# A new hand-written order and other load order in a kernel of two attention and MLP layers

## The chip, the cores and the metric

The kernel runs on one core of one Trainium2 chip. The metric is device time in microseconds; the value of a kernel is the median of its runs. Before the change it is 461.99 us, the median of 3 runs (460.26 to 463.19).

A core has five engines that run side by side, each through its own list of instructions in order: TensorE (PE in the profile, with its weight loads as PEld), VectorE (DVE), ScalarE (ACT), GpSimd (POOL) and SyncE (SP), which issues the transfers (DMAs) here. Engines wait for one another by semaphores.

## The reference, cut to what matters

One sequence of 2048 tokens with 512 features passes twice through an attention layer and an MLP layer, with the same weights both times. Everything is bfloat16.

```python
def _A_ref(x, wqkv, wo):
    H = 32; Dh = D // H; W = 256
    qkv = (x @ wqkv).reshape(B, S, 3, H, Dh).transpose(2, 0, 3, 1, 4)
    q, k, v = qkv[0], qkv[1], qkv[2]
    scores = jnp.einsum("bhqd,bhkd->bhqk", q, k) * (Dh ** -0.5)
    mask = (idx[:, None] - idx[None, :] >= 0) & (idx[:, None] - idx[None, :] < W)
    p = _softmax(jnp.where(mask[None, None], scores, -1e9), axis=-1)
    o = jnp.einsum("bhqk,bhkd->bhqd", p, v)
    return o.transpose(0, 2, 1, 3).reshape(B, S, D) @ wo

def _B_ref(x, w1, b1, w2, b2):
    h = _gelu(jnp.einsum("bsd,df->bsf", x, w1) + b1)
    return jnp.einsum("bsf,fd->bsd", h, w2) + b2

x = x + _A_ref(_layernorm(x), A_wqkv, A_wo)
x = x + _B_ref(_layernorm(x), B_w1, B_b1, B_w2, B_b2)
x = x + _A_ref(_layernorm(x), A_wqkv, A_wo)
x = x + _B_ref(_layernorm(x), B_w1, B_b1, B_w2, B_b2)
```

There are 32 heads of 16 features, a sliding window of 256 keys, and 1792 hidden features in the MLP. Without the structure of the window the projections, the output projection and the MLP hold most of the matrix work.

## The kernel before

**Tiles and stages.** The 2048 tokens are 16 tiles of 128; the two passes make 32 of them, and two tiles make a block, so there are 16 blocks. The residual stream stays in `X` on the chip, and so do all weights. For a tile, `layernorm` (line 932) takes statistics on VectorE (939 and 941), adds epsilon (943), takes the reciprocal root on GpSimd (946) and normalizes on VectorE (949). The normalized tile must then be transposed: early tiles on TensorE (36), with a copy out on VectorE (922) or ScalarE (924); later ones by a VectorE transpose of 32 x 32 pieces into `xs_` (958), four writes to a scratch tensor in memory (967) and one read back (973), into `xnTA` for attention or `xnTB` for the MLP. `by_dma` (565) says which tiles go that way. A read back waits until the last users of its buffer have finished.

`lnq` and `kv` (1006 and 1034) are a block's two LayerNorms and its projections from the Q, K and V blocks of `Wqkv_sb`. `attention` (1081) makes score visits: a visit is 16 or 24 small matmuls of 32 rows by 64 columns on TensorE, which run side by side on parts of the array, followed by two exponentials on ScalarE (1124). Masks (1145) run on VectorE or GpSimd, then come matmuls with V (64 rows by 17 columns), which also sum the softmax, then VectorE work (1210 to 1220) and the output projection (1245). `mlp` (1267) handles jobs of two or four tiles, `JOBS` at line 582. A block's keys also meet queries of the next block, so the first scores need the projection of block 1, that is of tiles 2 and 3.

TensorE is used in three ways: whole array (f), score pieces (r) and V pieces (c). ScalarE has to load another function table between exponential and gelu.

**What sets the order.** The code adds about 3,400 nodes to a planner, each with an engine, an estimated duration, what it reads and what it writes. A node may have a second form on another engine. The list `ORDER` (line 636) then gives the order by hand: each entry is a node's number, and a negative one (`-47`) means node `~(-47)`, that is 46, in its second form. `follow` (248) walks down the list and sets an estimated start for every node. With these estimates it picks the PSUM banks of each result, and the estimated times decide at two places what the program waits for and where: they rank the semaphore waits (`op`, 89), and `spread` (136) moves a second or third wait of a matmul onto an earlier matmul, when the estimate says that the event is past by then. Nothing else of the estimates reaches the chip. Each engine issues its nodes in list order.

**The loads.** Node 18 loads `X` tiles 0 and 1 (256 KB); 19, 20 and 22 are the K, Q and V blocks of the weight (512 KB each); 21 is `X` tiles 2 and 3 (256 KB); 23 is the first MLP bias; 24, 25 and 26 are the other tiles of `X`; 27 is the output weight, 28 the second MLP bias, 29 and 30 the MLP weights. The code adds them in that order of numbers. The order in which SyncE issues them is that of the list, which before the change has 18, 21, 20, 19, 22. `load` (883) gives each an estimated duration, from the time of its issue and its size.

Of the kernel before, what the change touches and what calls it, by code (L numbers as in the profile page):

```python
# [518 lines left out]
def bass_interleave_layers__sliding_block__dense_activation_gelu__prompt_kernel(  # L519
# [11 lines left out]
    Bb, S, D = A_x.shape  # L531
# [61 lines left out]
    with ExitStack() as kctx:  # L593
        S_ = _Sched(nc, kctx)

        def sb(name, shape, dtype=dt.bfloat16):
# [283 lines left out]
        sp_t = [0.0, 0.0]  # L880
        landing = {}

        def load(fn, writes, kb, issue=500.0, behind=()):

            i = sp_t[0]
            for n in behind:
# [42 lines left out]
        def quads(name):  # L929
            return ["%s_%d" % (name, q) for q in range(4)]  # L930
# [453 lines left out]
```

## Time and profile before

| | us |
|---|---|
| median of 3 runs | 461.99 |
| lowest, highest | 460.26, 463.19 |
| the profiled execution, its own time | 458.59 |
| its span from first to last instruction | 456.9 |

The granted clock of TensorE is 1.00 in all stretches. The 40 slices of the span show how the engines' shares move; each digit is a tenth of a slice of 11.4 us:

```profile
PE   7997899999889999999999999999999999999997
DVE  5999997889996888988989799998888878687302
ACT  2899999998998989899997999988978798875352
```

TensorE is nearly full from the second third on, ScalarE in the first third. The costliest groups are the exponentials and the two MLP matmuls; a group line has the kernel's line, the engine, what is written and read, the count, then the busy time and the mean duration in ns, and last the idle time before it:

```profile
L1124 ACT ACTIVATE E<-ps 128x1024 bf16<-128x1024 f32 x304 | 286.0, 1052 | 29.2 <-PE ps L32 28.3
L32 PE MATMUL ps<-W_sb,gT 128*128 128x512 bf16 (+1 forms) x462 | 117.7, 374 | 0.0
L32 PE MATMUL ps<-xnTB,W_sb 128*128 128x512 bf16 (+1 forms) x560 | 116.8, 337 | 0.0
```

Busy time of an engine is the union of its records. Matmuls overlap, so the mean of one is longer than the spacing between two.

### The profile page before, as it was taken

To read this page: it belongs to the slowest core of one execution; us is meant where nothing else is said; L and a number is where in the kernel's file an instruction comes from. 1 tells how busy PE (TensorE), PEld (TensorE's weight loads), DVE (VectorE), ACT (ScalarE), POOL (GpSimd) and SP (SyncE) were. 2 spreads that over 40 slices of the span, in tenths; PEclk is the share of its full clock that TensorE was granted. 3 is DMA by queue.
4 is the path that set the end of the run, shared out by engine and by line. 5 is a ranking of instruction groups with operands and counts; after the bars stand their busy time and mean duration, and the time that the engine had idled before them with its cause. 6 is when DMAs were issued, how large, how long until landed. Compare 5 with 4: busy or idle time off the path is not lost.

```text
span 456.9 us, 19399 instructions
## 1 busy us (share of the span) xinstructions
PE 438.8 (96%) x8738; PEld 233.2 (51%) x8738; DVE 374.2 (82%) x759; ACT 388.5 (85%) x463; POOL 221.8 (49%) x256
## 2 busy tenths in 40 slices
PE   7997899999889999999999999999999999999997
PEld 3564464654444444655435545545454554454675
DVE  5999997889996888988989799998888878687302
ACT  2899999998998989899997999988978798875352
POOL 5377665832668556562455536644434512270500
PEclk9999999999999999999999999999999999999999
DMA  7670000001031022402230122412130021003101
GB/s 230 215 261 3 4 4 3 4 3 37 6 66 29 16 39 61 70 14 42 46 75 8 23 42 47 87 16 51 25 87 13 6 46 37 26 3 84 57 24 46
DMA packets 63902, 22.35 MB, mean 49 GB/s; under 512 B 49740, under 2 KB 63308, under 8 KB 63820
## 3 DMA queue, kind: packets, MB, share of 16 engines
q1 hardware_dynamic: 63820, 21.12, 19.8%
q8 instruction: 68, 1.11, 1.0%
q14 instruction: 14, 0.11, 0.1%
HBM read 13.50 MB, written 7.60 MB: 46 GB/s over the span
## 4 chain that ended last, share of the span: by engine, by line
PE 71%; ACT 25%; DVE 2%; DMA 1%; issue 0%; SPq 0%; POOL 0%; DVEq 0%
PE ps L32 70%; ACT E L1124 18%; ACT gT L1291 2%; ACT gT L1282 1%; ACT L1124 1%; DMA scr_x<-xs_ 1%; ACT L1282 1%; DMA X<-in_A_x_dram 1%; DVE TT L1210 1%; PE ps L36 0%; DVE stat L939 0%; ACT QT L924 0%; ACT xnTA L924 0%; ACT L1291 0%; SPq L967 0%
## 5 line engine op out<-in xcount | busy, mean ns | idle before, releaser
L1124 ACT ACTIVATE E<-ps 128x1024 bf16<-128x1024 f32 x304 | 286.0, 1052 | 29.2 <-PE ps L32 28.3
L1145 POOL TENSOR_TENSOR E<-E,mask 128x512 bf16<-128x512 bf16 (+1 forms) x122 | 126.0, 1047 | 103.9 <-DVE E L1145 41.4
L32 PE MATMUL ps<-W_sb,gT 128*128 128x512 bf16 (+1 forms) x462 | 117.7, 374 | 0.0
L32 PE MATMUL ps<-xnTB,W_sb 128*128 128x512 bf16 (+1 forms) x560 | 116.8, 337 | 0.0
L32 PEld LDWEIGHTS ps<-xnTB,W_sb 128*128 128x128 bf16 x560 | 51.1, 98 | 43.6 <-ACT E L1124 3.5
L32 PE MATMUL ps<-xnTA,Wqkv_sb 128*128 128x256 bf16 x512 | 70.5, 273 | 2.5 <-DVE veps L943 1.6
L32 PE MATMUL ps<-QT,KT 32*64 32x320 bf16 (+4 forms) x2976 | 64.8, 258 | 7.4 <-ACT E L1124 5.4
L946 POOL TENSOR_TENSOR rstd<-veps,mhalf 128x1 f32<-128x1 f32 x64 | 36.7, 576 | 67.2 <-DVE veps L943 67.1
L1291 ACT ACTIVATE gT<-ps,b1T 128x512 bf16<-128x512 f32 (+1 forms) x92 | 48.7, 588 | 22.3 <-PE ps L32 22.1
L1003 DVE TENSOR_TENSOR X<-X,ps 128x512 bf16<-128x512 bf16 x63 | 42.7, 682 | 28.6 <-PE ps L32 28.1
L32 PEld LDWEIGHTS ps<-W_sb,gT 128*128 128x128 bf16 x462 | 40.8, 98 | 44.0 <-issue 5.7
L1145 DVE TENSOR_TENSOR E<-E,mask 128x512 bf16<-128x512 bf16 (+1 forms) x140 | 52.3, 406 | 11.0 <-ACT E L1124 10.6
L32 PEld LDWEIGHTS ps<-xnTA,Wqkv_sb 128*128 128x128 bf16 x512 | 46.5, 98 | 22.6 <-issue 3.3
L32 PEld LDWEIGHTS ps<-QT,KT 32*64 32x64 bf16 x2976 | 27.4, 103 | 53.9 <-ACT E L1124 35.4
L32 PE MATMUL ps<-E,Va 64*17 64x128 bf16 (+3 forms) x3872 | 49.3, 230 | 2.8 <-POOL E L1145 0.5
L32 PEld LDWEIGHTS ps<-E,Va 64*17 64x17 bf16 x3872 | 39.4, 85 | 21.0 <-PE ps L32 7.5
L1254 POOL TENSOR_TENSOR X<-X,b2b 128x512 bf16<-128x512 bf16 x32 | 36.7, 1153 | 22.5 <-DVE E L1145 11.5
L939 DVE BATCH_NORM_STATS2 stat<-X 128x6 f32<-128x512 bf16 x64 | 43.5, 684 | 2.8 <-DMA X<-in_A_x_dram 2.2
L1210 DVE STREAM_TRANSPOSE TT<-ps 128x1024 f32<-128x1024 f32 x32 | 39.8, 1243 | 6.0 <-PE ps L32 5.4
L1043 DVE TENSOR_TENSOR KT<-ps,parmask 128x1024 bf16<-128x1024 f32 x32 | 38.6, 1214 | 3.7 <-PE ps L32 3.5
L32 PE MATMUL ps<-Wo_sb,OT 128*128 128x512 bf16 x128 | 35.4, 381 | 0.1
L32 PE MATMUL ps<-Wqkv_sb,xnTA 128*128 128x512 bf16 x128 | 35.4, 381 | 0.0
(50 smaller groups left out, 319.4 us busy)
## 6 DMA issues: line engine op xcount, KB each, us to landing
W_sb<-in_B_w_dram SPq DMA_DIRECT2D x2, 1792.0 KB
scr_x<-xs_ SPq DMA_DIRECT2D x104, 32.0 KB, 1.6
xnTB<-scr_x SPq DMA_DIRECT2D x26, 128.0 KB, 2.7
scr_q<-xs_ SPq DMA_DIRECT2D x64, 32.0 KB, 2.2
xnTA<-scr_q SPq DMA_DIRECT2D x16, 128.0 KB
out_dram<-X SPq DMA_DIRECT2D x15, 128.0 KB, 1.8
Wqkv_sb<-in_A_wqkv_dram SPq DMA_DIRECT2D x3, 512.0 KB, 6.9
X<-in_A_x_dram SPq DMA_DIRECT2D x3, 512.0 KB, 5.7
```

What stands on the lines that cost most here:

```text
L32: return self.e.matmul(*a, **k)
L939: add("dve", lambda e, B: e.bn_stats(stat6[:, k6, :], X[:, t, :]), 590, reads=["X%d" % t], writes=["st%d" % k6], prio=prio)
L946: add("pool", lambda e, B: e.tensor_tensor(out=rstd[:, k : k + 1], in0=veps[:, k : k + 1], in1=mhalf[:], op=ALU.pow), 535, reads=["ve%d" % ...
L1003: add("dve", lambda e, B: e.tensor_tensor(out=X[:, t, :], in0=X[:, t, :], in1=ps[:, B[g][0], :], op=ALU.add), d_psum(512), reads=["X%d" % ...
L1043: add("dve", lambda e, B, g=g, i=i: e.tensor_tensor(out=KT[:, kb, :, 2 * i : 2 * i + 2, :].rearrange("p a c q -> p a (c q)"), in0=ps[:, B[ ...
L1124: add("act", lambda e, B, g_=g_, gi=gi: e.activation(E[:, 2 * gi : 2 * gi + 2, e0 : e0 + 512], ps[:, B[g_][0] : B[g_][0] + 2, :], AF.Exp, ...
L1145: op = lambda e, B, Ew=Ew, Mw=Mw: e.tensor_tensor(out=Ew, in0=Ew, in1=Mw, op=ALU.mult)
L1210: add("dve", lambda e, B: e.transpose(TT[:, s].rearrange("p a c q d -> p (a c q d)"), ps[:, B[g][0] : B[g][0] + 2, :].rearrange("p a n -> ...
L1254: add("pool", lambda e, B: e.tensor_tensor(out=X[:, t, :], in0=X[:, t, :], in1=b2b[:], op=ALU.add), 1110, reads=["X%d" % t, "b2b"], writes ...
L1282: add("act", lambda e, B, fcs=fcs: e.activation(gT[:, fcs[0] : fcs[-1] + 1, 0:M], gT[:, fcs[0] : fcs[-1] + 1, 0:M], AF.Gelu_apprx_tanh, sc ...
L1291: add("act", lambda e, B, g=g, fc=fc: e.activation(gT[:, fc, 0:M], ps[:, B[g][0], 0:M], AF.Gelu_apprx_tanh, bias=b1T[:, fc : fc + 1], scal ...
```

## The change

Three things change. The list `ORDER` is replaced by another one over the same nodes. In it the loads stand as 18, 19, 20, 21, 22: `X` 0 and 1, K, Q, `X` 2 and 3, V; and the output weight is loaded ahead of the second MLP bias. The estimate of a load no longer uses the higher price per KB between 0.2 and 3 us, and the K block gets an extra 1,300 ns. The estimates of the LayerNorm transfers grow: a scratch write from 3,700 to 4,300 ns in attention and from 2,700 to 3,100 in the MLP, a read back from 3,900 to 4,800 and from 3,300 to 3,900. The time for which an issue holds SyncE stays as it was in the estimate. Some nodes also change between their two forms.

```diff
         ORDER = [
-            8, 18, 15, 16, 9, 21, 10, 4, 20, 5, 3, 0, 19, 1, 11, 22, 2, 23, 40, 24, 41, 42, 33, 17, 43, 34, 35, 36, 44,
-            37, 45, 6, 38, 12, -47, 39, 13, 84, 62, 52, 53, 47, 85, 48, 86, 77, 49, 87, 50, 57, 78, -52, 58, 7, 79, 59,
...
+            0, 15, 16, 17, 18, 40, 4, 14, 5, 6, 19, 8, 20, 21, 1, 2, 22, 23, 9, 10, 11, 12, 3, 24, 41, 42, 43, 13, 33,
+            34, 35, 36, 7, 44, 45, 37, 38, 39, -47, 62, 57, 52, 53, 54, 63, 55, 58, 47, 48, 49, 50, 59, 84, 85, 86, 87,
...
-        def load(fn, writes, kb, issue=500.0, behind=()):
+        def load(fn, writes, kb, issue=500.0, behind=(), lag=0.0):
...
-            sp_t[1] = max(sp_t[1], i + 1900.0) + kb * (3.05 if i < 200 else 4.2 if i < 3e3 else 3.4) + (400.0 if behind else 0.0)
+            sp_t[1] = max(sp_t[1], i + 1900.0) + kb * (3.05 if i < 3e3 else 3.4) + lag + (400.0 if behind else 0.0)
...
-        load_qkv(1)
+        load_qkv(1, lag=1300.0)
...
-                        dur=2700.0 if layer else 3700.0, issue=500.0 if layer else 720.0)
+                        dur=3100.0 if layer else 4300.0, issue=500.0 if layer else 720.0)
...
-                    quads(dname), reads=["scr%d_%d_%d" % (layer, v, r) for r in range(4)], prio=prio, dur=3300.0 if layer else 3900.0, issue=400.0 if layer else 600.0)
+                    quads(dname), reads=["scr%d_%d_%d" % (layer, v, r) for r in range(4)], prio=prio, dur=3900.0 if layer else 4800.0, issue=400.0 if layer else 600.0)
```

More of the change, by code (lines that the diff above doesn't have):

```diff
@@ L896, in load_x, with load_qkv @@
                 ["X%d" % t for t in range(t0, t0 + n)], 128 * n, behind=behind)
-        def load_qkv(which):
+        def load_qkv(which, lag=0.0):
             load(lambda e, B: e.dma_start(
                 Wqkv_sb[:, :, which * D : (which + 1) * D],
-                A_wqkv[:, which * D : (which + 1) * D].rearrange("(c p) n -> p c n", p=P)), ["Wqkv%d" % which], 512)
+                A_wqkv[:, which * D : (which + 1) * D].rearrange("(c p) n -> p c n", p=P)), ["Wqkv%d" % which], 512, lag=lag)
         load_x(0, 2)
-        load_qkv(1)
+        load_qkv(1, lag=1300.0)
         load_qkv(0)
```

362 rows, old and new, of the table ORDER are left out of this document.

## The prediction, made before the changed kernel ran

> **What bounds the kernel now.** I read the list of busy times first, then the same sums over the stretches into which the chain of work falls, then that chain in order of time, the waits, and last the timeline of the first 16 us, where the moved loads act.
>
> ```profile
> span 456.9 us, 19399 instructions
> PE 438.8 (96%) x8738; PEld 233.2 (51%) x8738; DVE 374.2 (82%) x759; ACT 388.5 (85%) x463; POOL 221.8 (49%) x256
> ```
>
> ```profile
> 0.00:15.60 15.60, 12.32 (x89) 7.06 (x90) 10.42 (x24) 5.22 (x8) 5.96 (x22) 1.00 0.69 227
> 15.60:133.60 118.00, 107.40 (x2542) 61.74 (x2541) 108.36 (x236) 115.52 (x140) 70.82 (x75) 1.00 0.17 50
> 133.60:180.20 46.60, 45.55 (x986) 22.52 (x986) 37.72 (x72) 41.77 (x48) 31.37 (x33) 1.00 0.20 34
> 180.20:454.40 274.20, 273.50 (x5122) 141.82 (x5122) 217.25 (x429) 226.02 (x270) 113.61 (x126) 1.00 0.20 41
> ```
>
> ```profile
> 15.63 3.78 ACT E L1124 x4
> ...
> 125.23 8.36 ACT E L1124 x9
> 133.59 0.04 issue
> 133.64 4.83 PE ps L32 x169
> ...
> 172.98 0.47 SPq L967
> ...
> 180.22 81.23 PE ps L32 x1487
> ```
>
> The columns of the second block are the stretch, its length, then the busy time of PE, PEld, DVE, ACT and POOL, the granted clock, the DMA share and GB/s. There are three regimes. Up to the first exponential at 15.63 us the kernel waits for loads and the first LayerNorms. From there to 133.6 ScalarE is full: 115.52 of 118.00 us, so 2.48 idle, and the chain runs through its exponentials (8.36 us for 9, 0.93 each). From 133.6 on TensorE is full: idle 1.05 us to 180.2, and 0.70 (274.20 less 273.50) in the 274 us to 454.4. An order can win only in the head, in ScalarE's 2.48 us and in TensorE's 1.75; the matrix work itself stays.
>
> **The change part by part.** Counted in the issue order of both kernels, every engine does the same kinds of work: 304 exponentials, 18 table loads, 64 LayerNorms, 168 scratch writes, 42 reads back. Ahead of every fourth score visit the full-array matmuls placed on TensorE differ by at most 4 of 1890, the attention-times-V matmuls not at all. The new list is a shuffle within a few microseconds, not another plan.
>
> *The loads.* SyncE now issues X 0-1, K block, Q block, X 2-3, V block, where it had X 0-1, X 2-3, Q, K, V.
>
> ```profile
> 0.80 0.95 SPq L894 DMA_DIRECT2D X<-in_A_x_dram  x2
> 1.80 1.57 SPq L899 DMA_DIRECT2D Wqkv_sb<-in_A_wqkv_dram  x3
> 4.56 0.55 POOL L946 TENSOR_TENSOR rstd<-veps,mhalf 128x1 f32<-128x1 f32 x1 [1.66 <-DVE veps L943]
> 6.18 0.19 POOL L847 TENSOR_SCALAR_AFFINE_SELECT hot<-hot 128x8 f32<-128x8 f32 x1
> 6.34 0.30 POOL L860 TENSOR_TENSOR mask<-mask 128x64 bf16<-128x64 bf16 x1
> 6.59 0.60 ACT L924 ACTIVATE xnTA<-ps 128x512 bf16<-128x512 bf16 x1 [4.50 <-PE ps L36]
> 6.85 0.40 PE L36 MATMUL ps<-ident,xn 128*128 128x128 bf16 x4 [0.30 <-DVE xn L949]
> 7.29 0.42 DVE L922 COPY xnTA<-ps 128x512 bf16<-128x512 bf16 x1 [0.49 <-PE ps L36]
> 7.63 0.69 DVE L939 BATCH_NORM_STATS2 stat<-X 128x6 f32<-128x512 bf16 x1
> 8.85 3.00 PE L32 MATMUL ps<-xnTA,Wqkv_sb 128*128 128x256 bf16 x26 [1.60 <-DVE veps L943]
> 9.64 0.40 DVE L949 TENSOR_SCALAR xn<-X,statmv,rstd 128x512 bf16<-128x512 bf16 x1
> 10.41 0.91 POOL L865 MEMSET Va<- 128x192 bf16 x1
> 10.49 0.98 DVE L949 TENSOR_SCALAR xn<-X,statmv,rstd 128x512 bf16<-128x512 bf16 x1 [0.45 <-POOL rstd L946]
> 13.30 1.05 PE L32 MATMUL ps<-xnTA,Wqkv_sb 128*128 128x256 bf16 x8
> ```
>
> ```profile
> DMA to landing us min/median/max: 6.4/6.9/7.4
> ```
>
> The last row is that of the three weight blocks, issued some 0.5 us apart from 1.80. The first projection matmul needs the normalized tile, copied by 7.71, and the K block; it starts at 8.85. K went out last but one, at 2.31, and with the shortest landing, 6.4, it is there at 8.71: the real releaser, though the row names a VectorE instruction. In the new order K goes out at 1.30 and lands by 7.7 (the same 6.4, with half the bytes), so TensorE starts its projections at about 7.8, 1.05 us earlier. Q, out at 1.80, lands by 8.2 and is needed four matmuls in.
>
> But the first scores do not wait for these matmuls. They wait for block 1's query projection (13.30), which needs LayerNorm of tiles 2 and 3, and their load is now fourth. The transfer that was fourth, with the same 1.5 MB through its end, landed at 8.71; I take that for X 2-3. The statistics then start at 8.73 instead of 7.63. The first normalize comes as before 9.64 - 7.63 = 2.0 later, at 10.7, and ends at 11.1; a Q copy (some 0.7, as the statistics' 0.69 over as many elements) now stands before the second, which starts at 11.8. That one took 0.98 beside the 0.91 us memset on GpSimd; the memset now runs at the start, so it gets the first one's 0.40: done at 12.2, against 11.47. TensorE has by then done its 32 K and Q matmuls, one tile's transposes and two V matmuls (7.8 + 32 x 0.11 + 0.65 = 12.0; 0.11 is 3.00 us for 26). The second tile's transposes and ScalarE copy add 0.40 and 0.60, with hand-overs 1.2: query projection at 13.4 for 13.30. **Head: +0.1 us.** If X 2-3 lands before VectorE is free at 7.6, TensorE's 12.0 is the later one and the projection starts at 13.2: -0.1, and -0.3 if hand-overs vanish. If it takes the longest 7.4, landing at 9.7, the head costs +1.1. I stay with 8.71, the row with the same bytes ahead.
>
> [...]
>
> *GpSimd in the head.* Ahead of the first reciprocal root at 4.56 GpSimd was idle for 1.66 us. The new order puts 0.91 + 0.19 + 0.30 = 1.40 us of preparation there. It hides with 0.26 us to spare; beyond that cover it would go straight into the head. Wo and b2b swap places; no cost, since the first output projection comes long after.
>
> *ScalarE and VectorE.* Up to exponential 130 ScalarE loses one xnTA copy and gains one Q copy, 0.60 each: nothing where it bounds. Over the rest it has two more copies, VectorE over the whole five more instructions. Cover: 48 and 57 us idle under TensorE's 273.50. Without it, 2 x 0.60 + 5 x 0.69 = 4.7 us.
>
> *TensorE's turns between full-array, score and V work.* In the issue order they go from 366 to 371; three of the five come before score visit 57 of 152, under ScalarE's cover, two about visit 107, where TensorE bounds.
>
> ```profile
> 24.90 0.42 PE L32 MATMUL ps<-QT,KT 32*64 32x256 bf16 x16
> 25.26 1.48 PE L32 MATMUL ps<-xnTA,Wqkv_sb 128*128 128x256 bf16 x12
> 26.67 0.43 PE L32 MATMUL ps<-QT,KT 32*64 32x64 bf16 x24
> ```
>
> Twelve projections take 1.41 us to the next score, against 12 x 0.11 = 1.32: about 0.1 for that turn. The turn back lies somewhere in the 0.36 from 24.90 to 25.26. At 0.13, nearer to the measured end, the two are **+0.25 us**; bounds 0 and 5 x 0.36 = 1.8.
>
> *Transfers planned longer.* The larger durations alter no transfer, only which order fits the planner's clock, which PSUM banks it picks, and how early a semaphore wait may ride on an earlier matmul.
>
> ```profile
> DVE xs_ L958 <- DMA scr_x<-xs_: 0.5, 1, 0.5
> PEld ps L32 <- DMA xnTA<-scr_q: 0.4, 1, 0.4
> ```
>
> These are all the waits on LayerNorm transfers that the compute engines show: 0.9 us. More room wins at most that, and as TensorE idles only 1.75 us from 133.6 on, I put it at 0 (-0.9 to 0).
>
> *Sum.* +0.1 + 0.25 = +0.35 us on the profiled run's own 458.59 (span 456.9): 458.9. That run lies 3.4 below the median 461.99, so the median becomes **462.3**.
>
> **The rivals.** *Idle time goes (faster).* If the better-fitting order removes ScalarE's 2.48 us, TensorE's 1.75 and 0.3 in the head, the gain is 4.5: 462.0 - 4.5 = 457.5. Half of it, about 459.7, is likelier, for the same macro order leaves the causes in place: exponentials wait for score matmuls that stand behind the same projections.
>
> *SyncE's queue blocks (slower).* Reads back into the normalized tiles wait on SyncE until TensorE has freed the buffer, and all scratch writes of the next tiles stand behind them.
>
> ```profile
> SPq L973 <- PE ps L32: 13.3, 4, 6.9
> ...
> 109.61 1.71 PE L32 MATMUL ps<-E,Va 64*17 64x256 bf16 x128
> ...
> scr_x<-xs_ SPq DMA_DIRECT2D x104, 32.0 KB, 1.6
> xnTB<-scr_x SPq DMA_DIRECT2D x26, 128.0 KB, 2.7
> ```
>
> A tile's trip is four issues of 0.47, a landing of 1.6, an issue and 2.7: about 6.6 us. After the third tile of MLP job 3 (tiles 8 to 11) the new order leaves about 9.0 us of TensorE work before its first use: 34 projection matmuls of 0.11, 12 output matmuls of twice the width at 0.22, five score visits of 0.36, and 64 V matmuls, half of the 1.71. A block as long as the longest, 6.9, makes TensorE wait 6.9 + 6.6 - 9.0 = 4.5, so 466.8; two such, 471.3. It decides from a block of 2.4 us on. For it: SyncE's writes and reads are more interleaved than before. Against: counted the same way the room of most of the 42 tiles grew, on average by 1.8 us.
>
> *The loads do not do what they should.* X 2-3 lands at 9.7, and the head loses 1.1: 463.3.
>
> **How the numbers follow.** About 1% is what a measurement can tell from no change: 457.4 to 466.6. Even trade, 462.3 (460.7 to 463.9 by the bounds of head and turns): 0.58. Idle time goes: 0.22, a third of it beyond 1%. SyncE blocks: 0.15, two thirds beyond. Late X 2-3: 0.05. So faster 0.08, within 0.82, slower 0.10. The range takes in half the first rival's reach and the first blocked tile: 458.0 to 466.8.
>
> **What would show it.** First projection near 7.8 and first score within 0.5 us of 15.13 bear out the loads; a first score below 14.6 says that X 2-3 lands early. TensorE idle between 133.6 and 454.4 should stay near 1.75 us, ScalarE busy near 115.5 in the middle stretch. A new wait of SyncE on TensorE over 3 us with TensorE idle behind it is the slower rival; the same span with ScalarE idle gone is the faster one. The forecast is wrong if either stretch changes by more than 3 us.

## The result, and the profile after

| | before | after |
|---|---|---|
| median, us | 462.11 (460.26 to 464.57; 20 runs) | 460.34 (459.23 to 462.14; 20 runs) |
| profiled execution, us | 458.59, span 456.9 | 459.4, span 457.5 |

The ratio is 0.9961, 95% interval 0.9946 to 0.9976: 1.8 us less. The forecast was no change, 462.3. The two profiles say the opposite of the medians: after's span is 0.6 us longer. So the first thing to explain is not a line of after's profile but how either profile stands to its own runs.

The busy times of after, and the same four stretches as before (length, then busy PE, PEld, DVE, ACT and POOL, granted clock, DMA share, GB/s):

```profile
span 457.5 us, 19336 instructions
...
PE 431.0 (94%) x8664; PEld 234.5 (51%) x8738; DVE 376.6 (82%) x764; ACT 389.6 (85%) x465; POOL 217.4 (48%) x249
```

```profile
0.00:15.60 15.60, 12.36 (x90) 6.93 (x91) 10.56 (x26) 5.16 (x8) 5.84 (x22) 1.00 0.73 236
15.60:133.60 118.00, 106.17 (x2547) 62.98 (x2561) 109.52 (x241) 115.87 (x139) 66.12 (x72) 0.99 0.17 49
133.60:180.20 46.60, 44.79 (x987) 22.36 (x985) 40.93 (x80) 41.31 (x48) 25.55 (x27) 1.00 0.20 36
180.20:454.40 274.20, 267.11 (x5071) 141.97 (x5120) 214.83 (x420) 227.31 (x273) 119.87 (x129) 1.00 0.20 39
```

This trace lacks 74 matmul records (8664 for 8738 weight loads), so its TensorE time cannot be set against before's. A second profile of after, taken later, has all of them. Its rows for the second to fourth stretch:

```profile
15.60:133.60 118.00, 107.46 (x2565) 62.55 (x2563) 109.91 (x241) 116.10 (x140) 66.58 (x72) 1.00 0.18 50
133.60:180.20 46.60, 45.80 (x988) 22.48 (x987) 40.91 (x79) 41.31 (x49) 25.21 (x27) 1.00 0.20 36
180.20:454.40 274.20, 273.49 (x5100) 141.93 (x5098) 215.07 (x421) 226.77 (x273) 120.09 (x129) 1.00 0.20 40
```

Where the prediction looked for gains, little moved: ScalarE idles 1.90 us in the middle stretch (118.00 less 116.10) for 2.48 before, TensorE 0.80 and 0.71 in the last two for 1.05 and 0.70. That profile's span is 456.6, from its first exponential at 15.25 to the end 441.35; before's is 456.9, from 15.63 to the end 441.27. Behind the head these two executions take the same time to within 0.2 us.

The head of after in order of time, all engines:

```profile
1.24 4.49 PE L32 MATMUL ps<-gT 128*128 128x512 bf16 x11 [1.24 <-DVE gT L867]
1.29 0.99 SPq L899 DMA_DIRECT2D Wqkv_sb<-in_A_wqkv_dram  x2
...
2.33 0.51 SPq L894 DMA_DIRECT2D X<-in_A_x_dram  x1
...
4.88 0.55 POOL L946 TENSOR_TENSOR rstd<-veps,mhalf 128x1 f32<-128x1 f32 x1 [0.74 <-DVE veps L943]
...
7.96 3.23 PE L32 MATMUL ps<-xnTA,Wqkv_sb 128*128 128x256 bf16 x28 [0.52 <-DVE xnTA L922]
7.96 0.69 DVE L939 BATCH_NORM_STATS2 stat<-X 128x6 f32<-128x512 bf16 x1
...
10.91 0.40 DVE L949 TENSOR_SCALAR xn<-X,statmv,rstd 128x512 bf16<-128x512 bf16 x1
...
12.98 1.05 PE L32 MATMUL ps<-xnTA,Wqkv_sb 128*128 128x256 bf16 x8 [0.47 <-ACT xnTA L924]
...
14.71 0.42 PE L32 MATMUL ps<-QT,KT 32*64 32x256 bf16 x16
...
15.21 1.02 ACT L1124 ACTIVATE E<-ps 128x1024 bf16<-128x1024 f32 x1
```

The first projection is at 7.96 (forecast 7.8; before 8.85), and the statistics of X 2-3 start at once behind VectorE's copy, with no DMA named, so that load had landed by 7.96. The first score is at 14.71 for 15.13, the first exponential at 15.21 for 15.63: the head gained 0.42 where +0.1 was forecast. That is a quarter of the 1.8 us. The first row, 11 matmuls on a zeroed tile that nothing reads, turns out to matter more than all the others.

### The profile page after: what moved, and what is told of

The parts are those of the page before. It is cut to its first block, busy times and chain, and to the rows that moved or that the text cites. A ratio compares the mean times of both kernels' runs of the same rounds, so it can differ in the third digit from the quotient of the medians.

```text
span 457.5 us, 19336 instructions
## 1 busy us (share of the span) xinstructions
PE 431.0 (94%) x8664; PEld 234.5 (51%) x8738; DVE 376.6 (82%) x764; ACT 389.6 (85%) x465; POOL 217.4 (48%) x249
## 4 chain that ended last, share of the span: by engine, by line
PE 67%; ACT 25%; DVE 4%; issue 2%; DMA 1%; POOL 0%; DVEq 0%
PE ps L32 67%; ACT E L1124 16%; ACT gT L1291 4%; ACT gT L1282 2%; ACT L1124 1%; ACT L1291 1%; DVE TT L1210 1%; DVE stat L939 1%; DMA X<-in_A_x_dram 1%; ACT L1282 1%; DVE KT L1043 1%; ACT QT L924 0%; DVE E L1145 0%; PE ps L36 0%; ACT Va L924 0%
## 5 line engine op out<-in xcount | busy, mean ns | idle before, releaser
L1145 POOL TENSOR_TENSOR E<-E,mask 128x512 bf16<-128x512 bf16 (+1 forms) x117 | 123.9, 1071 | 101.2 <-DVE E L1145 36.9
L32 PE MATMUL ps<-W_sb,gT 128*128 128x512 bf16 (+1 forms) x420 | 105.2, 373 | 4.4 <-issue 3.7
L32 PE MATMUL ps<-xnTA,Wqkv_sb 128*128 128x256 bf16 x512 | 72.5, 277 | 3.0 <-DVE xnTA L922 0.8
L1145 DVE TENSOR_TENSOR E<-E,mask 128x512 bf16<-128x512 bf16 (+1 forms) x145 | 56.0, 413 | 8.3 <-ACT E L1124 8.1
L1279 DVE TENSOR_SCALAR gT<-ps,b1T 128x512 bf16<-128x512 f32 (+1 forms) x48 | 31.4, 670 | 5.7 <-PE ps L32 5.6
L32 PE MATMUL ps<-Wqkv_sb,xnTA 128*128 128x512 bf16 x110 | 31.1, 380 | 2.0 <-issue 1.3
```

The source lines that it names most:

```text
L32: return self.e.matmul(*a, **k)
L1145: op = lambda e, B, Ew=Ew, Mw=Mw: e.tensor_tensor(out=Ew, in0=Ew, in1=Mw, op=ALU.mult)
L1279: add("dve", lambda e, B, g=g, fc=fc: e.tensor_scalar(out=gT[:, fc, 0:M], in0=ps[:, B[g][0], 0:M], scalar1=b1T[:, fc : fc + 1], scalar2=No ...
```

## The experiments

Every median below stands beside runs of before in the same session; those have medians 461.07, 461.72, 462.35 and 462.31 in the four sessions. H, O, E and C in the expectations are theories: the head itself, the new order behind it, the longer planned durations, the granted clock of the head (the share of its full clock that TensorE is given there; the trace records it over time).

**A second profile of before.** No edit.

> The kernel before, unchanged, for a second profile of it: the profile that the prediction was made from came from an execution of 458.59 us, below every one of the kernel's 20 timed runs (460.26 to 464.57). Every theory expects a ratio of 1.000 within 0.002. What is asked is where a more usual execution spends the time: if the extra 2 to 3 us are a lower granted clock, the stalls of ScalarE (2.48 us idle from the first exponential to 133.6) and of TensorE (1.75 us idle after that) stay as they were and the matmuls lengthen; if they are stalls, they show in those two numbers.

Measured: ratio 1.0001 (0.9979 to 1.0024); the profiled execution took 462.1 us, span 460.4. TensorE's timeline of its head:

```profile
1.25 4.12 PE L32 MATMUL ps<-gT 128*128 128x512 bf16 x11 [1.25 <-DVE gT L867]
6.02 0.40 PE L36 MATMUL ps<-ident,xn 128*128 128x128 bf16 x4 [0.64 <-DVE xn L949]
7.01 0.40 PE L36 MATMUL ps<-ident,xn 128*128 128x128 bf16 x4 [0.59 <-DVE xn L949]
9.07 5.71 PE L32 MATMUL ps<-xnTA,Wqkv_sb 128*128 128x256 bf16 x26 [1.67 <-DMA Wqkv_sb<-in_A_wqkv_dram]
```

The 26 projections that took 3.00 us in the profile of the prediction take 5.71 here. In stretches, counting only the matmuls of line 32 (so without the transposes; length, PE, PEld, granted clock, DMA):

```profile
4.47:7.89 3.42, 0.90 (x4) 0.20 (x2) 1.00 0.99 303
7.89:11.30 3.41, 2.23 (x11) 1.60 (x12) 0.50 0.84 276
11.30:14.71 3.41, 3.41 (x17) 2.06 (x15) 0.50 0.47 148
```

TensorE is granted half its clock from 7.89 to 14.71 us. The first exponential comes at 18.55, 2.92 after that of the first profile, and the aligned exponentials of both traces stay 2.9 to 3.1 apart until 300 us. So the 3.4 us by which the prediction's profile undercut the median are for the most part this: that execution is one of the few in which the clock stayed full. Of 129 executions of before in these four sessions (one of 466.63 us aside) 19 have a mean clock of 1.000 (median 459.41), 54 one of 0.996 (461.18) and 56 one of 0.993 or less (462.54): no, one, two or more stretches of half clock, for a stretch of 3.41 us at 0.50 takes 0.0037 off the mean. The first class may hold more: an execution without a clock record is listed at 1.000 too, and so are four of the sixteen profiled ones.

**One part of the change at a time.** Before with the new load order alone:

```diff
-            8, 18, 15, 16, 9, 21, 10, 4, 20, 5, 3, 0, 19, 1, 11, 22, 2, 23, 40, 24, 41, 42, 33, 17, 43, 34, 35, 36, 44,
+            8, 18, 15, 16, 9, 19, 10, 4, 20, 5, 3, 0, 21, 1, 11, 22, 2, 23, 40, 24, 41, 42, 33, 17, 43, 34, 35, 36, 44,
```

> Before with the new load order alone (X 0-1, K, Q, X 2-3, V); the order of all other work is before's. Theory H (the 1.8 us come from the head, through the loads): the first projection moves from 8.85 to about 8.0, the first score from 15.13 to about 14.7, and the time falls to some 461.0 to 460.3. Theory O (the new order of the work behind the head brings it): the head may move by up to 0.4 us, but the time stays at 462.1, within 0.5. Because before's order still does the block-0 normalizing before the copies it was planned with, a head no earlier than 15.1 is possible too; then the loads bring something only together with the new order.

Measured: 459.53 us, ratio 0.9964 (0.9944 to 0.9985): all of the gain. But at full clock the head did the reverse of what theory H wanted. TensorE:

```profile
8.04 3.07 PE L32 MATMUL ps<-xnTA,Wqkv_sb 128*128 128x256 bf16 x26 [0.52 <-DVE xnTA L922]
...
15.88 0.42 PE L32 MATMUL ps<-QT,KT 32*64 32x256 bf16 x16
```

The first projection is 0.8 earlier and the first score 0.74 later than in before's first profile, since X 2-3 landed at 9.02 and before's order still has the 0.91 us memset beside the second normalize, which takes 0.97 there and 0.40 in after. From the first exponential to 300 us its exponentials stay 0.72 to 0.77 behind those of that profile, and its execution took 459.48 for 458.59: in this pair, both at full clock, the new load order costs time. So the kernel's lower median does not come from a shorter path in the head. What differs is the clock: the 12 mean clocks are 1.000 (seven) and 0.996 (five), none lower, and the five took 458.93 to 460.37, no more than the seven, so none of them shows the price that 0.996 has in before. Through the planner the swap also changes the PSUM banks of 3 steps; the constant lag shows no effect of that.

After with the old load order (the same swap the other way):

> After with the old load order (X 0-1, X 2-3, Q, K, V), all else as after. Theory H: K comes last but one again, the first projection starts near 8.85, the first score slips from 14.71 to about 15.1 or later, and the whole gain goes: 462.1. Theory O: the head gives back its 0.4 us at most and the time stays at 460.3 to 460.8.

Measured: 462.12, ratio 1.0017 (0.9995 to 1.0040): the gain is gone. The mean clock is below 1.000 in 9 of 12 executions, and the eight of them at 0.996 took 461.72 to 463.09; in the profile it is 0.50 from 8.67 to 12.09, and the first exponential is at 17.47.

After with the old planned durations:

```diff
-            sp_t[1] = max(sp_t[1], i + 1900.0) + kb * (3.05 if i < 3e3 else 3.4) + lag + (400.0 if behind else 0.0)
+            sp_t[1] = max(sp_t[1], i + 1900.0) + kb * (3.05 if i < 200 else 4.2 if i < 3e3 else 3.4) + (400.0 if behind else 0.0)
...
-                        dur=3100.0 if layer else 4300.0, issue=500.0 if layer else 720.0)
+                        dur=2700.0 if layer else 3700.0, issue=500.0 if layer else 720.0)
```

> After's order of the work and of the loads with the old, shorter estimates of the load and scratch transfers. The order of instructions and the PSUM banks are then the same as in after; only the places of some of TensorE's semaphore waits can differ. Theory E (the estimates themselves do something at run time, through those waits): the time moves back toward 462.1. Theories H and O: 460.3, within 0.4.

Measured: 460.34, ratio 0.9987 (0.9964 to 1.0011). The median is after's own to the hundredth, as H and O had it. But before was fast in that session (461.07), and the interval takes in 1, so E is not excluded by it, and no other run tests E alone. Theory C is the one taken up next.

**The clock itself.** The stretches of the clock record are 3.41 us or multiples of it (6.83, 122.88, 327.68, 450.56). The record begins with the first grant of full clock, at 3.90 to 6.97 us depending on the execution; the zero matmuls start 0.43 us apart until then and 0.22 after. What follows goes with the work in the 3.41 us behind that grant. For three executions, the matmuls of line 32 in that stretch and in the next. Before's first profile:

```profile
6.71:10.12 3.41, 1.27 (x12) 1.17 (x13) 1.00 1.06 345
10.12:13.54 3.42, 3.01 (x26) 2.16 (x25) 1.00 0.19 58
```

After:

```profile
5.21:8.62 3.41, 1.17 (x9) 0.60 (x7) 1.00 1.09 357
8.62:12.04 3.42, 3.31 (x27) 2.34 (x25) 1.00 0.41 129
```

After's order with the old durations:

```profile
4.37:7.78 3.41, 0.98 (x6) 0.23 (x4) 1.00 1.07 356
7.78:11.20 3.42, 3.42 (x17) 2.42 (x18) 0.50 0.67 214
```

With 0.98 us of such work full clock is lost, with 1.17 it is kept. All twelve profiles with a record divide so: kept at 1.17, 1.18, 1.27, 1.35, 1.38, 1.52 and 2.38, lost at 0.64, 0.72, 0.81, 0.90 and 0.98. With the transposes counted they don't (kept at 1.67, lost at 1.77). The border was read off these twelve; the runs below test its direction, more zeros or fewer, and not its value. For these heads the border lies between 0.98 and 1.17 us of such work in 3.41; why it is the matmuls without the transposes that divide them, and why the clock falls at all, no trace here shows.

Such a border would also explain the load order. In before TensorE's zeros end by 5.4 to 6.1, and K lets the projections start at 8.85 to 9.07: by the author's estimate from these times, the 3.41 us behind most first grants then hold less than 1.1 us of work. In after the projections start at 7.96, and only grants between about 4 and 5.2 us have too little behind them (an estimate from the profiles with after's head: the grant at 4.37 had, those at 3.90 and 5.21 had not). If that is right, the number of zero matmuls alone must move the time, up and down. After again, unchanged, and with 13 and with 9 of them; before with 16:

```diff
         for h in range(NZ):
-            PL.root = (add("pe", (clear, lambda e, B: clear(e, B, 3))[h], (16, 6)[h] * mm(512), reads=["zero", "g0"], writes=["ps:init0", "ps:init1"], prio=-200, geo="f"),)
+            PL.root = (add("pe", (clear, lambda e, B: clear(e, B, 5))[h], (16, 6)[h] * mm(512), reads=["zero", "g0"], writes=["ps:init0", "ps:init1"], prio=-200, geo="f"),)
```

(8 + 5 = 13; 8 + 1 = 9; 8 + 8 = 16, and later 8 + 6 = 14.)

> After, unchanged, once more, beside the three kernels below. Theory C (the granted clock of the head): the profiles so far show one stretch of half clock (0.50 for 3.41 or 6.83 us, starting at 7.8 to 8.7 us) in four of the executions of before and of after's order, and none in others; what decides is whether TensorE does enough matmul work in the 3.41 us after its first grant of full clock. After should show mean clocks of 1.000 and 0.996 about equally, where before shows 0.996 and 0.993, and a median near 460.3, with executions near 459.5 (no half clock in the head) and near 461.7 (one stretch). Theory H (head and order shorten the path by themselves, the clock being noise that hits both alike): the same share of half clock as in before, and a shift of all executions by the same 1.8 us.

> After with 13 instead of 11 matmuls on zeros at the start. Theory C: after's remaining executions with half clock in the head (about a third of them, near 461.7) go, and the median falls to 459.5 to 459.8; what remains are the undisturbed executions, delayed by at most 0.3 us where the transposes have to wait for the added matmuls. Theory H: 460.3, or slower by the added matmuls.

> After with 9 instead of 11 matmuls on zeros. Theory C: the work ends at about 5.1 us, the stretch after the first grant is then too empty for most phases, half clock follows in most executions, and the median rises to 461.5 to 463, at least to before's. Theory H: two matmuls on zeros less, that nothing waits for: 460.3 or a little less.

> Before with 16 instead of 11 matmuls on zeros at the start; nothing else, loads and order as before. Theory C: TensorE works until about 6.0 to 7.4 us instead of 5.4 to 6.1, so the stretch after the first grant has 1.1 us or more of matmul work whatever the phase of the clock's windows, no half clock follows, and the time falls by as much as after's or more: 459.2 to 459.8, all clocks at 0.996 or more. The K block still lands at 8.7, so the extra matmuls delay nothing by more than some 0.3 us. Theory H: the extra work on zeros hides nothing and brings nothing: 461 to 462, or more.

| kernel | median, us | ratio to before | mean clock below 1.000 |
|---|---|---|---|
| after | 460.10 | 0.9977 (0.9954 to 1.0001) | 2 of 12 |
| after, 13 zeros | 459.06 | 0.9961 (0.9941 to 0.9980) | 3 of 12 |
| after, 9 zeros | 464.00 | 1.0051 (1.0031 to 1.0071) | 8 of 9 |
| before, 16 zeros | 460.23 | 0.9987 (0.9965 to 1.0008) | 3 of 12 |

Two matmuls on zeros fewer, and after is slower than before; two more, and it has the lowest median so far. The directions are theory C's, the sizes less so: 459.06 lies below the expected 459.5 to 459.8, 464.00 above 461.5 to 463, and after, expected with a mean clock of 0.996 in about half of its executions, shows it in 2 of 12. (The expectation counts four heads with half clock; three of the six profiles kept until then show one.) TensorE's timeline with 13 zeros, then with 9:

```profile
1.24 5.73 PE L32 MATMUL ps<-gT 128*128 128x512 bf16 x13 [1.24 <-DVE gT L867]
6.76 0.72 PE L36 MATMUL ps<-ident,xn 128*128 128x128 bf16 x8
8.00 3.23 PE L32 MATMUL ps<-xnTA,Wqkv_sb 128*128 128x256 bf16 x28 [0.52 <-DVE xnTA L922]
```

```profile
1.23 3.45 PE L32 MATMUL ps<-gT 128*128 128x512 bf16 x9 [1.23 <-DVE gT L867]
...
8.01 4.57 PE L32 MATMUL ps<-xnTA,Wqkv_sb 128*128 128x256 bf16 x28 [0.52 <-DVE xnTA L922]
```

The added zeros push the transposes together but do not move the first projection; the removed ones cost 4.57 - 3.23 = 1.34 us of half clock at the same start. That is only part of the rise of 3.9 us. In the profile with 9 zeros the exponentials lag those of after's second profile by 1.35 us up to 80 us, by 1.71 at 113 and by 5.27 at 160: between these a second stretch of half clock (130.25 to 133.67) and two standstills of TensorE, 0.77 and 1.12 us, add to the late head. Eight of the nine executions have a mean clock of 0.992 or 0.993, that is two stretches. The clock column undercounts: executions without a record count as full clock, and both profiled ones with 16 zeros are such. Before with 16 zeros missed its expected 459.2 to 459.8 by half a microsecond; two more runs, below, took that up.

**Splices.** To see whether after's order behind the head carries anything, after's loads and first 143 positions were put before the rest of before's order, and the reverse; then the first with 13 zeros, and after with 13 a second time.

> After's loads and after's order for the first 143 of the 3375 positions (through the first exponentials), before's order for all that follows; 11 matmuls on zeros. Theory C (the head and its granted clock are all of the difference): as after, median 460.0 to 460.5, first exponential near 15.2 where the clock stays full, and 441.3 us from there to the end as in before. Theory O (the new order behind the head carries part of the 1.8 us): 460.8 to 461.7.

> The complement: before's loads and before's order for the first 155 positions, after's order for all that follows. Theory C: the first projection is back at 8.9 to 9.1, half clock follows as often as in before, and the median is 461.5 to 462.5. Theory O: some of the gain stays, 460.5 to 461.2.

> As the first of these, with 13 matmuls on zeros instead of 11. Theory C: as after with 13 of them (459.06): 458.9 to 459.5, below the first of these by about 1 us. If after's order behind the head has a stall of its own that before's has not (three profiles of after's order show 1.4 us at about 138 us that others do not), then up to 0.4 us less than with after's order.

> After with 13 matmuls on zeros, a second time, beside the others: 459.0 to 459.4, at or under 0.997 of before.

Measured: 464.09 (ratio 1.0044, 1.0022 to 1.0066), 463.99 (1.0042, 1.0012 to 1.0072), 465.30 (1.0075, 1.0042 to 1.0107); and 459.06 (0.9944, 0.9921 to 0.9968). The three splices missed: they are slower than both kernels and tell nothing of the question. The third has the good head, first exponential at 15.35 with full clock, is still 0.27 us ahead of before's first profile at 125 us, and ends 7.8 behind it. A hybrid order gets other PSUM banks from the planner (some 130 of 3375 steps differ from before in the first), and TensorE waits longer for exponentials; that the banks are the reason was not tested apart. The waits of TensorE's matmuls from 130 to 454 us (in total, times, longest) in the first splice:

```profile
PE ps L32 <- ACT E L1124: 4.4, 9, 1.2
PE ps L32 <- ACT gT L1291: 0.9, 2, 0.5
```

and in before:

```profile
PE ps L32 <- ACT E L1124: 0.8, 3, 0.4
```

What is left for the question is the profiles themselves. From the first exponential to the end, after's order took 441.35 us above and 441.8 in both profiles with 13 zeros; before's order took 441.27 above, 441.8 in its second profile, 441.4 with the new loads, and 442.1 and 442.8 with 14 and 16 zeros below. The executions scatter by more than the two orders differ, so no gain behind the head is shown, and one of half a microsecond could not be seen. The fourth run confirms the 13 zeros.

**Before with 14, and with 16 again.**

> Before with 14 instead of 11 matmuls on zeros, beside 16 of them once more. Theory C by its own rule (of the profiles so far, full clock was kept where the 3.41 us after the first grant held at least 1.17 us of matmuls other than the transposes, and lost at 0.97 or less): 14 last long enough for grants up to about 4.9 us and after some 6.2 us, not between, so half clock goes from most executions of before but not from all: a median of 460.0 to 461.0, between before and 16. Theory H: 461.5 to 462.5.

> Before with 16 matmuls on zeros, a second time, for a profile with a clock record. It measured 460.23 where 459.2 to 459.8 was expected, and the profile had 1.7 us of TensorE waiting for one LayerNorm transfer at 295 us, beside 0.23 us in the head. If that wait is chance, this profile lacks it, ends within 1 us of before's 456.9, and the median is 459.5 to 460.3; if the later head causes it, it is there again.

Measured: 459.98 (ratio 0.9968, 0.9946 to 0.9989) and 460.55 (0.9967, 0.9951 to 0.9983). Before, with its own loads and its own order, gets all that the change brought from three matmuls on zeros more. TensorE in the head with 14:

```profile
1.25 5.67 PE L32 MATMUL ps<-gT 128*128 128x512 bf16 x14 [1.25 <-DVE gT L867]
...
8.84 3.00 PE L32 MATMUL ps<-xnTA,Wqkv_sb 128*128 128x256 bf16 x26 [1.31 <-DVE statmv L941]
...
15.13 0.42 PE L32 MATMUL ps<-QT,KT 32*64 32x256 bf16 x16
```

Projection and score stand where they stood in the prediction's profile, 8.85 and 15.13. This execution has no clock record, but its 26 projections take 3.00 us, as they did there at full clock, for 5.71 at half. The wait of 1.7 us at 295 us is not in the second profile of 16 zeros (span 458.7), so the later head alone does not bring it. The first exponential of that profile is at 15.92, 0.29 later than before's. Both its median and its span lie above what was expected (460.3 at most; within 1 us of 456.9); 0.3 us of that is the later start (the K block landed at 9.00 for 8.71), the rest stays open. One of its twelve executions took 882.01 us; nothing on record says why, and the median without it is 460.53.

## Why the prediction was wrong

*The step that failed* is the last of the sum: "That run lies 3.4 below the median 461.99, so the median becomes 462.3." It treated 3.4 us as an offset that any kernel has. It is a cost of before's head that this profile happened not to show, and the edited loads act on it. The prediction listed the clock at 1.00 in all four stretches and drew no question from it, though the three timed runs (460.26 to 463.19) all lay above the profiled 458.59. So the signs that it named came true (first projection near 7.8, first score within 0.5 us of 15.13, ScalarE busy near 115.5, TensorE idle near 1.75, no new block of SyncE), and the time still went another way: they all look at the path, none at the clock.

By what was measured, before's executions lie on average (54 x 1.77 + 56 x 3.13) / 129 = 2.1 us above their full-clock 459.41 (1.77 and 3.13 are the distances of the medians 461.18 and 462.54). That is the cost that the prediction took for an offset; 0.8 of its 3.4 is something else, the distance of the profiled 458.59 from that 459.41. After's 32 executions have no mean clock below 0.996; of the eleven at 0.996 five took 459.40 to 459.75, as if it cost them little, and six 461.42 to 462.77. What stays open is the rest of the account: the 19 of after at 1.000 have a median of 459.96, above before's 459.41, though its head is 0.42 shorter at full clock. So the runs show that the gain comes with the lost half-clock stretches, not how the 1.8 us add up.

*Loads.* K earlier and the first projection near 7.8: borne out (7.96). What was missed is the second thing an early K does: it shortens the hole between zeros and projections. The prediction weighed K only by what waits for it.

*X 2-3 "to land at 8.71".* In after it was there by 7.96, in the load swap alone at 9.02, in a splice at 9.79 and in another at 8.35: the forecast value was a fair middle of what scatters by at least 1.8 us from one execution to the next. The size of the head, +0.1 for the measured -0.42, is not the landing's doing: with 13 zeros the statistics start at 8.51, 0.55 later than in after, and the query projection still at 13.01 for 12.98. The second tile's transposes start at 11.94 and 11.90, though in after that tile is normalized by 11.31: there TensorE's own work is the later one, which is the prediction's other branch (-0.1 to -0.3; the query projection moved by 0.32). The last 0.1 lies between the query projection and the first score, 1.73 us for 1.83, which the forecast had left as it was.

*GpSimd's preparation.* Hidden, as forecast: the first root comes at 4.88 after 0.74 idle.

*Turns, ScalarE's and VectorE's extra instructions, planned durations.* Forecast +0.25, 0, 0; together 441.35 less 441.27, +0.1, which two executions cannot tell from 0, nor from the forecast.

*Rivals.* No new block of SyncE: its waits for TensorE at the reads back sum to 13.7 us in five, the longest 5.0, for 13.3 in four and 6.9, and no TensorE idle follows. The idle time of ScalarE and TensorE went down by 0.6 and 0.2 us; the rival's size for half of it, 459.7, came near the time for another reason, which is luck. None of the rivals was the right mechanism, so their chances rested on the wrong list. The range's lower end, 458.0, does not follow from its own words either: half of the first rival's reach is 459.7.

## What to carry to other kernels

Before a forecast is set against a median, ask whether the profiled execution is a usual one: compare its time and its granted clock with those of the timed runs. Where TensorE starts on dummy work and then waits for its first load, look at the matmul time within 3.4 us of the first full grant; here a hole that left 0.98 us or less of it cost half clock, and 1.17 or more kept full clock; which it was went with the time of the grant, so the time is a mixture, and a change pays by its chance of closing the hole as well as by the path it shortens. Padding the dummy work until the first operand lands is a cheap cure to try: here 13 for 11 in the new order, 459.06 us in both sessions, the lowest median of all that ran, though by their ratios before with 14 (0.9968) and the new loads alone (0.9964) are not told apart from it.

## What the runs showed of the hardware beyond that

The clock falls away from the head too. In the first profile of after 3.41 us of half clock follow a stretch with 1.88 us of PE time, in the ScalarE-bound part:

```profile
124.67:128.09 3.42, 1.88 (x80) 0.88 (x63) 3.39 (x6) 3.36 (x4) 0.00 (x0) 1.00 0.41 66
128.09:131.50 3.41, 3.21 (x29) 1.76 (x28) 3.00 (x7) 3.21 (x5) 0.01 (x1) 0.50 0.35 83
```

By the exponentials of both profiles of after it cost 0.5 us there, against 1.3 or more in the head. Two more profiles lose the clock in that part, after 1.83 us (9 zeros) and 1.76 (the third splice). All three are above the 1.17 that sufficed in the head, so the head's border does not carry over. Score and V matmuls, on parts of the array, are in the mix here, but in the splice 1.36 us of the work was on the whole array; why the clock falls stays open.

TensorE can also stand still with nothing to wait for that the profile shows. After's order with the old durations, at 140 us:

```profile
138.27 0.65 PE L32 MATMUL ps<-E,Va 64*17 64x256 bf16 x41
140.06 0.35 PE L32 MATMUL ps<-E,Va 64*17 64x192 bf16 x27 [1.13 <-issue]
```

The same gap, 1.12 to 1.19 us at the same place of the order, is in the four profiles with after's order and a late head, and in none with an early one; in each it ends 1.40 to 1.45 us after a 16 KB instruction packet has landed (here at 138.61), which in the others is there by 136.2. So a late head goes with 1.4 us more there in after's order; in the six profiles of before's order as it stands no such gap of TensorE reaches 0.6 us behind the head. That the packet is the cause was not tested, nor why it starts late; shorter gaps of the kind, 0.67 to 0.85 us at about 126 us, stand in profiles with an early head too.
